# A decode step with adaLN: the closing rows in two column groups, with two plain stores

## The chip, the cores and the metric

The kernel runs on one core of a Trainium2 chip. The metric is device time of one execution in microseconds (us), taken over several executions of each kernel; lower is better. A profiled execution of each kernel gives a trace. The span of a profile (84 us here) is shorter than the device time (85.7 us) by what lies before the first and after the last instruction.

## The reference

One token for each of four sequences goes through an attention block with a key and value cache and through a feed-forward block, both with an adaptive layer norm:

```python
mod = (silu(c) @ w_mod).reshape(4, 6, 1, 512)              # sa, ca, ga, sb, cb, gb
h = layernorm(x) * (1 + ca) + sa
x = x + ga * attention(h, k_cache, v_cache, wq, wo)        # 32 heads, window of 1024 keys
h = layernorm(x) * (1 + cb) + sb
x = x + gb * (relu(h @ w1) @ w2)                           # w1: 512 x 1792, w2: 1792 x 512
```

The output is 4 x 512 in bf16, 4 KB. The inputs that have to be read are 32 MB.

## The kernel before

The change concerns the last line of the reference. The sum over 1792 is cut in 14 blocks of 128 (block m, `w2_sb[:, m, :]`), and w2 arrives in five loads, of 4, 4, 3, 2 and 1 blocks. The activation of a block, `uT32[:, m, :]`, is a 128 x 32 weight tile with the four sequences in columns 0, 8, 16 and 24 and zeros between. Each block takes four matmuls, one in each group of 32 columns of the array; group g makes output columns 128 g to 128 g + 127 and leaves them on partitions 32 g to 32 g + 31.

```python
CG = 32; NH = 4; DH2 = 128; BS = 8
W2_CHUNKS = [(0, 4), (4, 4), (8, 3), (11, 2), (13, 1)]
...
def ffn2(m0, m1):
    for m in range(m0, m1):
        for nh in range(NH):
            nc.tensor.matmul(out=z_ps[nh * CG:(nh + 1) * CG, :], lhsT=uT32[:, m, :],
                             rhs=w2_sb[:, m, nh * DH2:(nh + 1) * DH2],
                             start=(m == 0), stop=(m == FT - 1), tile_position=(0, nh * CG))
...
nc.vector.tensor_tensor(out=zg[:], in0=z_ps[:], in1=gb2[:], op=ALU.mult)
nc.vector.tensor_tensor(out=res[:], in0=zg[:], in1=x12_ps[:], op=ALU.add)
nc.scalar.dma_start(out=out.rearrange("b o (g n) -> (o g) b n", g=NH), in_=res[::BS, :])
```

So the 16 rows to be stored lie on every eighth partition, and their places in the output need two dimensions, [4 groups, 4 sequences], beside the 256 bytes of a row.

## Time and profile before

| | before |
|---|---|
| device time, median of the first 3 runs | 85.74 us (85.63 to 85.79) |
| span of the profile | 84.19 us |
| last landing of w2 | 80.62 us |
| last matmul ends | 80.96 us |
| store issued, landed | 81.66 us, 83.36 us |

The first two rows are the whole; the other three are single records of the trace and cut the piece that the change can touch. The page's clock row belongs to it, since the last matmuls run at the throttled clock (each digit is a fortieth of the span, in tenths of full speed):

```profile
PEclk9999999999996555599999999559755555555555
```

And these are the w2 matmuls of the kernel before in order of time (start, duration, engine, line, what, count, idle time before and what ended it):

```profile
78.25 1.10 PE L472 MATMUL z_ps<-w,uT 128*32 128x128 bf16 x32 [0.21 <-DVE uT L467]
...
79.66 0.51 PE L472 MATMUL z_ps<-w,uT 128*32 128x128 bf16 x12 [0.31 <-DMA w<-in_B_w_dram]
...
80.33 0.64 PE L472 MATMUL z_ps<-w,uT 128*32 128x128 bf16 x12 [0.15 <-DMA w<-in_B_w_dram]
```

The reader is to see the gaps: the tensor engine is through with what has landed and waits for the next load of w2 (0.31 us, then 0.15 us).

### The profile page before, as it was taken

The numbers are of one execution on the slowest core, as the hardware profiler recorded it, in microseconds if no ns is written. First come the engines' busy times: TensorE is split into PE (matmuls) and PEld (weight loads), VectorE is DVE, ScalarE is ACT, GpSimd is POOL, SyncE is SP. The second block draws the span as 40 slices with busy tenths as digits, with TensorE's granted clock in tenths as the row PEclk, the third lists the DMA queues.
The fourth block names the chain that finished last, engine by engine and source line by source line (L and its number), as shares of the span: only waits on it lengthen the run. The fifth ranks groups of instructions, "written<-read, shape, count | busy, mean of one in ns | idle before, by whom it ended". The sixth has DMA issues, their size and how long they took to land.

```text
span 84.2 us, 2368 instructions
## 1 busy us (share of the span) xinstructions
PE 56.2 (67%) x1064; PEld 47.2 (56%) x1064; DVE 25.7 (31%) x73; ACT 23.6 (28%) x37; POOL 5.2 (6%) x20
## 2 busy tenths in 40 slices
PE   0001006999972889999999941999727579598730
PEld 0000006996772883997777801999727239588610
DVE  0104000348133100164665476950001320251320
ACT  2301001664302000487788718640100010001000
POOL 6980000000000000000000000000000000000000
PEclk9999999999996555599999999559755555555555
DMA  2799999999989999999999999999999999999500
GB/s 31 301 457 455 386 432 471 459 483 420 389 370 405 424 424 424 401 428 424 409 420 420 420 420 416 416 424 428 409 416 424 416 415 432 418 387 399 186 1 2
DMA packets 4221, 32.14 MB, mean 382 GB/s; under 512 B 492, under 2 KB 628, under 8 KB 1268
## 3 DMA queue, kind: packets, MB, share of 16 engines
q1 hardware_dynamic: 4176, 31.98, 91.7%
q8 instruction: 8, 0.13, 0.6%
q10 hardware_dynamic: 36, 0.01, 0.1%
q14 instruction: 1, 0.01, 0.0%
HBM read 31.99 MB, written 0.00 MB: 380 GB/s over the span
## 4 chain that ended last, share of the span: by engine, by line
DMA 93%; SPq 2%; PE 1%; DVE 1%; issue 0%
DMA v<-in_A_v_cache_dram 33%; DMA wo_sb<-in_A_wo_dram 24%; DMA w<-in_B_w_dram 19%; DMA k<-in_A_k_cache_dram 16%; PE z_ps L472 1%; SPq L81 1%; SPq L91 0%; SPq L90 0%; DVE zg L482 0%; DVE res L484 0%
## 5 line engine op out<-in xcount | busy, mean ns | idle before, releaser
L204 PE MATMUL ktp<-ident_k,k 128*128 128x128 bf16 x256 | 19.1, 247 | 6.5 <-DMA k<-in_A_k_cache_dram 6.5
L204 PEld LDWEIGHTS <-k 128*128 128x128 bf16 x256 | 18.1, 113 | 9.1 <-DMA k<-in_A_k_cache_dram 6.6
L209 ACT COPY kT<-ktp 128x1024 bf16<-128x1024 bf16 x16 | 15.6, 1015 | 19.0 <-PE ktp L204 18.0
L207 DVE COPY kT<-ktp 128x1024 bf16<-128x1024 bf16 x16 | 11.1, 692 | 18.0 <-PE ktp L204 17.7
L342 PE MATMUL oT_ps<-pT,v 128*128 128x16 bf16 x256 | 7.1, 172 | 2.0 <-issue 2.0
L342 PEld LDWEIGHTS <-v 128*128 128x128 bf16 x256 | 7.0, 100 | 2.1 <-issue 2.0
L216 PE MATMUL sc_ps<-kT,qpad 128*32 128x512 bf16 x64 | 5.6, 445 | 0.4 <-DVE qpad L308 0.4
L359 PE MATMUL pT_ps<-ident_bf,p_rep 128*128 128x128 bf16 x32 | 3.2, 282 | 2.9 <-DVE p_rep L353 2.9
L179 PE MATMUL tp<-ident_bf,cx_sb 8*128 8x8 bf16 x4 | 0.3, 169 | 6.6 <-DMA cx_sb<-in_A_x_dram 6.6
L359 PEld LDWEIGHTS <-p_rep 128*128 128x128 bf16 x32 | 2.8, 131 | 3.4 <-DVE p_rep L353 3.4
L304 PE MATMUL qT_ps<-hT,wq_sb 128*128 128x4 bf16 x128 | 3.5, 166 | 1.4 <-DVE ab L297 1.4
L304 PEld LDWEIGHTS <-wq_sb 128*128 128x128 bf16 x128 | 3.5, 104 | 1.5 <-issue 1.5
L179 PEld LDWEIGHTS <-cx_sb 8*128 8x128 bf16 x4 | 0.2, 112 | 6.6 <-issue 6.6
L411 ACT COPY y<-y_ps 128x256 f32<-128x256 f32 x1 | 0.4, 372 | 9.3 <-DVE y L410 9.3
L353 DVE TENSOR_TENSOR p_rep<-e_sb,mi 128x512 int32<-128x512 int32 x4 | 2.5, 687 | 0.7 <-ACT e_sb L348 0.7
L472 PE MATMUL z_ps<-w,uT 128*32 128x128 bf16 x56 | 2.2, 303 | 0.7 <-DMA w<-in_B_w_dram 0.5
L384 DVE TENSOR_TENSOR oT_sb<-oT_ps,rb 128x128 bf16<-128x128 f32 x1 | 0.3, 291 | 7.8 <-PE oT_ps L342 7.8
L418 PEld LDWEIGHTS <-wo_sb 128*128 128x128 bf16 x64 | 2.5, 120 | 0.4 <-DMA wo_sb<-in_A_wo_dram 0.4
L418 PE MATMUL y_ps<-o,wo_sb 128*128 128x4 bf16 x64 | 2.4, 173 | 0.3 <-DMA wo_sb<-in_A_wo_dram 0.3
L414 PEld LDWEIGHTS y_ps<-sel_b,y 128*128 128x128 f32 x8 | 1.8, 327 | 1.4 <-DVE y L410 1.4
L406 PE MATMUL y_ps<-wo_sb,o 128*32 128x512 bf16 x16 | 1.9, 628 | 0.9 <-DVE o L397 0.9
L216 PEld LDWEIGHTS <-qpad 128*32 128x32 bf16 x64 | 1.3, 103 | 2.2 <-DVE qpad L308 0.7
(107 smaller groups left out, 51.9 us busy)
## 6 DMA issues: line engine op xcount, KB each, us to landing
k<-in_A_k_cache_dram SPq DMA_DIRECT2D x8, 1024.0 KB, 28.1
v<-in_A_v_cache_dram SPq DMA_DIRECT2D x8, 1024.0 KB, 20.1
wq_sb<-in_A_wq_dram SPq DMA_DIRECT2D x1, 4096.0 KB, 22.5
wo_sb<-in_A_wo_dram SPq DMA_DIRECT2D x4, 1024.0 KB, 20.4
wmod_sb<-in_w_mod_dram SPq DMA_DIRECT2D x1, 2304.0 KB, 9.7
w<-in_B_w_dram SPq DMA_DIRECT2D x1, 1792.0 KB, 21.9
w<-in_B_w_dram SPq DMA_DIRECT2D x2, 512.0 KB, 19.5
wmod_sb<-in_w_mod_dram SPq DMA_DIRECT2D x1, 768.0 KB, 4.6
```

The lines of the kernel that those rows point to most:

```text
L204: nc.tensor.transpose(out=tp[:, ii, :], in_=k_tiles[gi][:, iq * IQ + ii, :], identity=ident_k)
L207: nc.vector.tensor_copy(out=dst, in_=tp[:])
L209: nc.scalar.copy(out=dst, in_=tp[:])
L216: nc.tensor.matmul(out=sc_ps[hw * CG:(hw + 1) * CG, half * HALF:(half + 1) * HALF], lhsT=qpad[:, b, par, hw, :], rhs=kT[:, half * (NI // 2 ...
L304: nc.tensor.matmul(out=qT_v[:, hq, :], lhsT=wq_sb[:, t, hq * Dh:(hq + 1) * Dh], rhs=hT[:, t, :], start=(t == 0 and hq == 0), stop=(t == DT ...
L342: nc.tensor.matmul(out=oT_ps[:, hw, par].rearrange("p b r -> p (b r)"), lhsT=v_tiles[h][:, i, :], rhs=pT[:, i, c0:c0 + B * rep], start=(fi ...
L353: nc.vector.tensor_tensor(out=p_w[:, ws, :], in0=e_w[:, ws].unsqueeze(2).to_broadcast([P, WQ // 2, B]), in1=mi4[:].unsqueeze(1).to_broadca ...
L359: nc.tensor.transpose(out=tp[:, ii, :], in_=p_rep[:, i // 2, :, i % 2], identity=ident_bf[:])
L406: nc.tensor.matmul(out=y4_ps[q0:q0 + CG, :], lhsT=o4[:, l, g % 2, g // 2, :], rhs=wo_sb[:, g, l, :], start=(g == 0 and l < 4), stop=(g == ...
L414: nc.tensor.matmul(out=y_ps[:, t, :], lhsT=y4[:, t, :], rhs=sel_b[:], start=(t == 0), stop=False)
L418: nc.tensor.matmul(out=y_ps[:, m, :], lhsT=wo_sb[:, g, l, m::DT], rhs=o4[:, l, g % 2, g // 2, 0:B], start=False, stop=(g == NP - 1 and l = ...
L472: nc.tensor.matmul(out=z_ps[nh * CG:(nh + 1) * CG, :], lhsT=uT32[:, m, :], rhs=w2_sb[:, m, nh * DH2:(nh + 1) * DH2], start=(m == 0), stop= ...
```

## The change

The intent is a cheaper store. If a group's 32 columns hold the four sequences at columns 0, 2, 4, 6 once and at 1, 3, 5, 7 once (the same tile, read from one column earlier: windows x = 0 and 1), the group can make two output quarters on interleaved, adjacent partitions. Two groups then suffice, the result lies on partitions 0 to 7 and 32 to 39, and two stores with plain patterns, one on SP's queue and one on ACT's, take it out. To make up for the two idle groups, blocks 0 to 3 of w2 go to the upper two groups, beside blocks 4 to 7 in the lower ones, and their part is copied, scaled and added to the residual ahead of time (zc). The core of the diff; the same windows are used for gb and x12 earlier, which is cut here:

```diff
-    siluT32 = const.tile([P, DT, CG], bf16, name="siluT32")
+    siluT32 = const.tile([P, DT, CP], bf16, name="siluT32")       # CP = CG + 2; uT32 and xs2 likewise
+    def rows(tile3, j, x):
+        return tile3[:, j, NX - x:NX - x + CG]                    # NX = 2
+    def closing(parts):
+        for x in range(NX):
+            for (ps, q, j, src, rhs, start, stop, cols) in parts:
+                for g in range(2):
+                    q0 = (q + g) * CG
+                    nc.tensor.matmul(out=ps[q0:q0 + CG, cols], lhsT=rows(src, j, x), rhs=rhs(2 * x + g),
+                                     start=start and x == 0, stop=stop and x == NX - 1, tile_position=(0, q0))
 ... (cut)
-    for (m0, e) in W2_CHUNKS:
-        ffn2(m0, m0 + e)
+    for m in range(ZA):                                           # ZA = 4
+        closing([zpart(m), zpart(ZA + m)])                        # upper groups beside lower groups
+    zc = work.tile([2 * CG, DH2], f32, name="zc")
+    nc.scalar.copy(out=zc[:], in_=za_ps[2 * CG:P, :])
+    nc.vector.tensor_tensor(out=zc[:], in0=zc[:], in1=gb2[:], op=ALU.mult)
+    nc.vector.tensor_tensor(out=zc[:], in0=zc[:], in1=x12_ps[:], op=ALU.add)
+    for m in range(2 * ZA, FT):
+        closing([zpart(m)])
 ... (cut)
-    nc.vector.tensor_tensor(out=res[:], in0=zg[:], in1=x12_ps[:], op=ALU.add)
-    nc.scalar.dma_start(out=out.rearrange("b o (g n) -> (o g) b n", g=NH), in_=res[::BS, :])
+    nc.vector.tensor_tensor(out=res[:], in0=zg[:], in1=zc[:], op=ALU.add)
+    out_v = out.rearrange("b o (x g n) -> (b o x) g n", x=NX, g=2)
+    nc.sync.dma_start(out=out_v[:, 0, :], in_=res[0:NX * B, :])
+    nc.scalar.dma_start(out=out_v[:, 1, :], in_=res[CG:CG + NX * B, :])
```

## The prediction

> **What bounds the kernel now.** I read the page's engine shares first, then its slices, then the chain that ended last in order of time, and last the trace of the final four microseconds. No engine is full, so the bound is not a compute engine:
>
> ```profile
> PE 56.2 (67%) x1064; PEld 47.2 (56%) x1064; DVE 25.7 (31%) x73; ACT 23.6 (28%) x37; POOL 5.2 (6%) x20
> ...
> DMA  2799999999989999999999999999999999999500
> ...
> HBM read 31.99 MB, written 0.00 MB: 380 GB/s over the span
> ```
>
> The DMA row stands at 9 from the third slice to the thirty-seventh: the kernel streams 32 MB of caches and weights, and everything else lies beside that stream. The chain says the same and shows what lies outside:
>
> ```profile
> 64.37 15.92 DMA w<-in_B_w_dram
> 80.28 0.04 issue
> 80.33 0.66 PE z_ps L472 x11
> 80.99 0.02 issue
> 81.01 0.30 DVE zg L482
> 81.31 0.02 issue
> 81.34 0.29 DVE res L484
> ```
>
> Up to 80.28 us the chain is DMA alone. So a change of this kernel that reads the same bytes can pay only in the piece from the last landings of w2 to the end at 84.2 us, about 4 us of 84. The reader is to see that line 472's matmuls, two vector instructions and the store follow each other there, nothing beside them. The store and the wait for it take most of it:
>
> ```profile
> 81.66 0.60 ACTq L485 DMA_DIRECT2D out_dram<-res  x1
> ```
>
> ```profile
> SPq L511 <- DMA out_dram<-res: 1.6, 1, 1.6
> ```
>
> The second line is from the waits of the DMA queue's engine: it waits 1.6 us for the store, up to 83.37; the remaining 0.8 us, to 84.19, is the closing hand-shake of the engines, which the change doesn't touch. From single records: the last five loads of w land at 77.39, 78.69, 79.62, 80.28 and 80.62 (issue time plus time to landing: the last is 66.85 plus the 13.8 of the page's DMA part). The matmuls wait for the last one, start at 80.66 and end at 80.96; zg runs 81.01 to 81.30, res 81.34 to 81.62; the store is issued from 81.66 to 82.26, its first packet starts at 82.91, its last at 83.02, and it has landed at 83.36.
>
> **What the Trainium skill says.** (1) "TensorE: Matmul & The Clock Gate", "Wait — 56ns, not 53.3ns?": at the throttled clock matmuls follow each other every N / 1.2 GHz, 106.7 ns for 128 columns. The trace agrees: in this stretch the granted clock is 0.50, and in the run of line 472 from 78.25 rounds of four matmuls (one in each column group) start 105 to 107 ns apart. (2) Same page, "Part 3: Packing small matmuls", "The mechanism": matmuls at different tile positions run beside each other, about 4 ns apart. The trace agrees: the four of a round start within 3 to 16 ns. So a column group takes one matmul in 107 ns, and with two groups in use the array has half the throughput of four. (3) "VectorE: DVE Perf Modes", section on the TRN2 errata: an fp32 tensor-tensor instruction takes (N+151)/0.96 ns, and that does not depend on how many partitions it covers. At N = 128 this is 291 ns; zg took 292 and res 287. (4) "DMA: Bandwidth & Descriptors", "Why a DMA increments its semaphore by 16 and not by 1": the number of DMA engines is the largest common divisor, up to 16, of the two patterns' slowest dimensions. The store's [4,4] destination makes it 4, and its 16 packets of 256 bytes indeed come four to an engine; five semaphore events (one for the unused twelve, four landings) agree. An [8] by 256 byte store should use 8 engines with one packet each.
>
> **The change, part by part.** In the front part little is at stake. The widened zero tiles and the small copy ident_m cost 0.2 us of DVE and some ns of POOL, both idle there until 6.6 us. Gb's 16 matmuls in two groups cost PE at most some 0.3 us in the early stage, and x12 keeps its 16 matmuls; the loads are issued 14 to 28 us before they land, so such a shift leaves the stream as it is. After x12, PE waits for w1 anyway (landed 76.12, first u matmul 76.17; x12 ended at 75.74), a slack of 0.4 us. These parts: 0.
>
> W2's first 32 matmuls (blocks 0 to 3 beside 4 to 7) use all four groups again, so the pace is the same; but the first pair needs the second chunk, landed 78.69, where before it was needed only half-way. Eight rounds by 107 ns from 78.73 end their starts at 79.59, just ahead of the third chunk (79.62, start 79.66): 0, with no slack left. The ACT copy of za_ps (gb's like copy took 251 ns) and two vector instructions (about 290 each) begin near 79.9 and are over by 80.8, ahead of zg: 0.
>
> From block 8 on only two groups work, and here the change loses. Blocks 8 to 10 are 12 matmuls = 6 rounds by 107 ns: 79.66 to 80.30, about when the fourth chunk lets PE go on (80.33). Blocks 11 and 12 are 4 rounds, not 2; from the spacing of the trace (the second round of a burst follows after about 65 ns, the later ones after 107) the next round could start at about 80.71, after the last landing and its 80.66. The last block takes 2 rounds and not 1: 80.71 + 0.107 + 0.31 (one matmul's record) = 81.13, against 80.96. **PE on the path: +0.17 us.**
>
> The final vector pair is unchanged in length: same 128 columns, half the partitions, zc from SBUF in place of x12_ps; the trace's 128x16 instructions take 174 ns from either memory. So 0, and res ends near 81.79.
>
> The stores: the old one is issued on ACT in 602 ns with the pattern [4,4]. SP's issues show what a second dimension costs: loads of k and v, pattern [1,128], take 535 ns, wo and w, pattern [128,1], take 328. ACT's second load at the start, [4,1], took 265. I take 328 on SP and 265 to 400 on ACT, side by side: −0.27 us. Then the packets: four to an engine from 82.91 to 83.02 become one to an engine and queue, −0.06 us (estimate from 18 ns a packet and 11 to 15 ns spacing). One more semaphore to await at the end: +0.03. **Stores on the path: −0.30 us.** Sum: 0.17 − 0.30 = −0.13 us, span 84.06, time 85.74 − 0.13 = **85.6 us**.
>
> **The rivals.** (a) The issue does not get cheaper. For it: ACT's very first issue, also two-dimensional, took 568 ns, and at that moment SP was issuing too; if it was the simultaneous issue or the long pause of the queue that made it slow, the ACT store will take 0.57 again. Against: SP's issue at that same moment took 374, little over its 328. Then only −0.03 and −0.06 + 0.03 remain, and with PE's +0.17 the time is 85.8 to 85.9. (b) PE's loss is larger: weights of both windows go to the same two groups, and if a weight load can't hide behind a matmul of its own group, a round takes more than 107 ns. The trace speaks against it (four groups each took a new weight load in every 107 ns round), but with the 12 + 8 + 4 matmuls of the last six blocks each 10 ns costs 0.12 us: 86.0. (c) PE's loss is hidden. If the last landing comes later than 80.71 in a typical run, the queue of earlier blocks is empty by then and only one extra round (0.107) is left: 85.5. (d) The landing of a 4 KB store is dominated by its receipt, 0.35 us after the last packet and 0.65 between issue and first packet, so the finer split gains nothing beyond the issue: 85.7. A gain in the stream is no rival: same bytes, same order of loads.
>
> **Range and chances.** The pieces run from −0.40 (stores all gained, PE half hidden) to +0.25 (issue not cheaper and PE's loss full). Runs of the kernel before spread by 0.16 us, another chip may shift all by a tenth or two. I take 85.2 to 86.0. Two per cent is 1.7 us, nearly half of the whole closing piece that the change can touch; no chain of these pieces comes near. Within 2%: 0.97; faster 0.02; slower 0.01.
>
> **What would show it.** Right: the last landing within 0.1 us of 80.6; line 194's last z_ps matmul ending 0.45 to 0.55 us after that landing (0.34 before); the records of the last six blocks in rounds of two, 107 ns apart; zg and res still about 290 ns; two store issues starting within 50 ns of each other, both under 0.4 us; one data packet to an engine and queue; end of span 0.82 us after the later landing. Wrong: an issue near 0.57 or 0.6 us on ACT (rival a); rounds of more than 115 ns (b); last z_ps matmul starting 43 ns after the landing (c); zc's sum ending after the last matmul, which would put ACT and DVE on the path; a wait of the u matmuls for x12 in place of w1.

## The result, and the profile after

The changed kernel takes 85.81 us (median of 6 runs, 85.68 to 85.95), the kernel before 85.73 us in the same rounds (6 runs, 85.61 to 85.98). Ratios here are the mean time of one kernel's fast runs over that of the other's of the same rounds, so not quite the ratio of the medians; this one is 1.0007, with a 95% interval of 0.9989 to 1.0025: the same.

The chain of the changed kernel in order of time, its last pieces:

```profile
79.44 1.48 PE z_ps L194 x26
80.95 0.29 DVE zg L504
81.27 0.28 DVE res L506
```

Where the chain of the kernel before came from DMA to a burst of 11 matmuls of 0.66 us, it now ends in 1.48 us of matmuls whose records leave no gap: the tensor engine has become the last link in this stage. A matmul's record lasts 0.31 us, so records overlap and hide short waits. By the starts of the single records the engine still waited for the fourth load, which landed at 80.045 and was used from 80.086; the six rounds from there to the end wait for nothing. (Further up this chain goes through PE from 13 to 39 us, where the other went through DMA. That is a matter of which of two waits ended last; the DMA row of the page is full there in both kernels, and w2's last landing is at 80.36 us, no later than before.) The timeline of the same piece:

```profile
79.22 1.68 PE L194 MATMUL z_ps<-w,uT 128*32 128x128 bf16 x26
...
79.49 0.26 ACT L497 COPY zc<-za_ps 64x128 f32<-64x128 f32 x1 [3.57 <-PE za_ps L194]
79.78 0.28 DVE L498 TENSOR_TENSOR zc<-zc,gb 64x128 f32<-64x128 f32 x1 [1.31 <-ACT zc L497]
80.10 0.28 DVE L499 TENSOR_TENSOR zc<-zc,x_ps 64x128 f32<-64x128 f32 x1
80.95 0.28 DVE L504 TENSOR_TENSOR zg<-z_ps,gb 64x128 f32<-64x128 f32 x1 [0.57 <-PE z_ps L194]
81.27 0.28 DVE L506 TENSOR_TENSOR res<-zg,zc 64x128 bf16<-64x128 f32 x1
81.58 0.37 SPq L508 DMA_DIRECT2D out_dram<-res  x1
81.58 0.30 ACTq L509 DMA_DIRECT2D out_dram<-res  x1
```

To see: zc is ready at 80.38, well ahead of zg at 80.95, where VectorE waits for the tensor engine; the two issues start together and take 0.37 and 0.30 us in place of 0.60. So the store side is cheaper, as intended. The total did not move because two things took it back. I cut the piece after the last landing of w2 in five parts, from single records of the traces:

| us | last landing of w2 to last matmul's end | to the first store's issue | to the last store's landing | to SP's first closing drain | to the end | sum |
|---|---|---|---|---|---|---|
| before | 0.342 | 0.693 | 1.699 | 0.083 | 0.751 | 3.568 |
| changed | 0.544 | 0.666 | 1.397 | 0.248 | 0.750 | 3.605 |
| difference | +0.202 | −0.027 | −0.302 | +0.165 | −0.001 | +0.037 |

The third column is what the change is for. The first is the price at the tensor engine. The fourth was not foreseen at this size: after its store has landed, SP works through a fixed sequence of waits for all semaphores of the kernel, mostly two to an instruction. In the kernel before the store's semaphore is in the last of these; the changed kernel has one DMA more, which moves SP's store to the third, so that three further waits, about 0.06 us each, run after the landing: the wait for SP's store ends at 82.995 us, three more start at 83.031, 83.093 and 83.152, and the drain at 83.220 (single records of the trace, which no view prints).

The last landing itself moves from run to run (80.10 to 80.62 us over the profiles, with no relation to the kernel that I can see), and so the times scatter by some 0.3 us. The five parts are steadier: the kernels that share a part agree in it within 0.03 us, but for D where the stores' semaphores are the last two (waits_last). I use the parts for the mechanism and the ratios for the whole.

### The profile page after: what moved, and what is told of

It is laid out like the page before. It is cut to its first block, busy times and chain, and to the rows that moved or that the text cites. A ratio compares the mean times of both kernels' runs of the same rounds, so it can differ in the third digit from the quotient of the medians.

```text
span 84.0 us, 2373 instructions
## 1 busy us (share of the span) xinstructions
PE 55.5 (66%) x1064; PEld 46.5 (55%) x1064; DVE 26.5 (32%) x76; ACT 23.8 (28%) x38; POOL 5.3 (6%) x20
## 4 chain that ended last, share of the span: by engine, by line
DMA 60%; PE 30%; DVE 3%; issue 1%; SPq 1%; ACT 1%; DVEq 0%
DMA v<-in_A_v_cache_dram 24%; DMA w<-in_B_w_dram 23%; DMA k<-in_A_k_cache_dram 14%; PE ktp L225 14%; PE qT_ps L322 4%; PE sc_ps L237 3%; PE z_ps L194 3%; PE mT L273 2%; PE mT L275 1%; PE m_ps L259 1%; PE m_ps L262 1%; PE st_ps_var L289 1%; PE gb_ps L194 1%; SPq L93 0%; SPq L92 0%
## 5 line engine op out<-in xcount | busy, mean ns | idle before, releaser
L225 PE MATMUL ktp<-ident_k,k 128*128 128x128 bf16 x256 | 17.8, 237 | 7.5 <-DMA k<-in_A_k_cache_dram 7.5
L225 PEld LDWEIGHTS <-k 128*128 128x128 bf16 x256 | 16.8, 108 | 10.1 <-DMA k<-in_A_k_cache_dram 7.5
L194 PEld LDWEIGHTS <-uT 128*32 128x32 bf16 x56 | 2.2, 136 | 0.8 <-DMA w<-in_B_w_dram 0.4
```

Source lines behind the costliest of these rows:

```text
L194: nc.tensor.matmul(out=ps[q0:q0 + CG, cols], lhsT=rows(src, j, x), rhs=rhs(2 * x + g), start=start and x == 0, stop=stop and x == NX - 1, ...
L225: nc.tensor.transpose(out=tp[:, ii, :], in_=k_tiles[gi][:, iq * IQ + ii, :], identity=ident_k)
```

## The experiments

Twelve runs followed the first result; waits_again is the kernel of waits_last once more. This is the same cut for each, one profiled execution each; the texts below refer to its columns as A to E. The diffs are shortened in places, and say so:

| us | A: landing to matmul's end | B: to store's issue | C: to store's landing | D: to SP's drain | E: to the end | sum | ratio to before (95%) |
|---|---|---|---|---|---|---|---|
| before | 0.342 | 0.693 | 1.699 | 0.083 | 0.751 | 3.568 | 1 |
| changed | 0.544 | 0.666 | 1.397 | 0.248 | 0.750 | 3.605 | 1.0007 (0.9989 to 1.0025) |
| late4 | 0.339 | 0.657 | 1.387 | 0.247 | 0.745 | 3.375 | 0.9962 (0.9940 to 0.9984) |
| lower_only | 0.815 | 0.665 | 1.391 | 0.247 | 0.745 | 3.863 | 1.0045 (1.0019 to 1.0071) |
| waits_last | 0.548 | 0.667 | 1.380 | 0.143 | 0.745 | 3.483 | 0.9973 (0.9954 to 0.9993) |
| before_2x3d | 0.342 | 0.688 | 1.920 | 0.247 | 0.751 | 3.948 | 1.0043 (1.0017 to 1.0069) |
| one_store | 0.540 | 0.665 | 1.187 | 0.084 | 0.745 | 3.221 | 0.9960 (0.9936 to 0.9985) |
| both_act | 0.543 | 0.668 | 1.534 | 0.248 | 0.744 | 3.737 | 1.0034 (1.0002 to 1.0067) |
| before_joined | 0.338 | 0.691 | 1.725 | 0.143 | 0.745 | 3.642 | 1.0010 (0.9987 to 1.0034) |
| chunks_last | 0.853 | 0.664 | 1.384 | 0.084 | 0.751 | 3.736 | 1.0006 (0.9984 to 1.0028) |
| chunks_fine | 0.838 | 0.673 | 1.391 | 0.084 | 0.750 | 3.736 | 1.0005 (0.9988 to 1.0023) |
| waits_again | 0.555 | 0.665 | 1.384 | 0.084 | 0.745 | 3.433 | 0.9975 (0.9958 to 0.9992) |
| before_4x2d | 0.338 | 0.689 | 2.773 | 0.395 | 0.750 | 4.945 | 1.0155 (1.0137 to 1.0173) |
| pattern_split | 0.550 | 0.668 | 2.064 | 0.248 | 0.750 | 4.280 | none: one run, 86.71 us, state unknown |

### late4: four column groups to the end (wrong)

```diff
     for m in range(2 * ZA, FT):
-        closing([zpart(m)])
+        for x in range(NX):
+            for g in range(2):
+                j = 2 * x + g; q0 = j * CG        # window 1 goes to the upper groups of zb_ps, never read
+                nc.tensor.matmul(out=(zb_ps if x else z_ps)[q0:q0 + CG, :], lhsT=rows(uT32, m, x), ...)   # (cut)
```

> The changed kernel, but from block 8 on the second window's matmuls go to the two upper column groups of a tile that nobody reads: four groups stay in use to the end. The result is wrong on purpose; the stores, the vector work and the closing waits are those of the changed kernel. Theory (the two-group matmuls lose, the stores win back as much): from the last landing of w2 to the end of the last matmul 0.34 us as in the kernel before, in place of 0.54; the piece from last landing to the end of the span 3.40 us in place of 3.60; time about 0.2 us under the changed kernel, near 85.6. Rival (the matmuls' pace is not what lengthened this piece, but later weight loads or the start of the last block): it stays above 0.45 us and the time stays at 85.8.

The last z_ps matmuls of this kernel, and the vector instruction that follows them:

```profile
80.02 0.29 PE L506 MATMUL z_ps<-w,uT 128*32 128x128 bf16 x2 [0.17 <-DMA w<-in_B_w_dram]
...
80.31 0.29 PE L506 MATMUL z_ps<-w,uT 128*32 128x128 bf16 x2
...
80.64 0.28 DVE L510 TENSOR_TENSOR zg<-z_ps,gb 64x128 f32<-64x128 f32 x1 [0.35 <-PE zb_ps L506]
```

The engine waits for the fourth load again (0.17 us), and the last load, landed at 80.267, is used from 80.31 on. A is 0.339 us, the kernel before's 0.342; the sum falls by 0.230 to 3.375, and the time to 85.41 us, lower than the 85.6 expected. The number of matmuls and weight loads is that of the changed kernel, only the groups differ. So the 0.2 us is the pace of two groups, and the rest of the change, taken alone, gains.

### lower_only: without the early upper groups

```diff
-        upper = m < ZA
+        upper = False        # (cut: the tile za_ps goes, start and stop are m == 0 and m == FT - 1)
-    for m in range(ZA):
-        closing([zpart(m), zpart(ZA + m)])
-    ... zc ...
-    for m in range(2 * ZA, FT):
+    for m in range(FT):
         closing([zpart(m)])
-    nc.vector.tensor_tensor(out=res[:], in0=zg[:], in1=zc[:], op=ALU.add)
+    nc.vector.tensor_tensor(out=res[:], in0=zg[:], in1=x12_ps[:], op=ALU.add)
```

> The changed kernel without its early upper groups: all 14 blocks of w2 in the two lower groups, no za_ps, zc and copy, the sum with x12 from PSUM as before. Theory (a group takes one matmul in 107 ns): the 56 matmuls are 28 rounds from about 78.0, 3.0 us, so the last one starts near 80.95 and ends near 81.25, 0.3 to 0.35 us later than in the changed kernel after the same landings; time about 86.1. Rival (PE catches up, since it waits for w2 anyway): the last matmul ends as in the changed kernel, time 85.8.

The timeline of this kernel, its w2 matmuls:

```profile
78.05 3.17 PE L194 MATMUL z_ps<-w,uT 128*32 128x128 bf16 x56 [0.16 <-DVE uT L484]
```

All 56 matmuls in one run, with no wait for w2 in between: 28 rounds by 107 ns are 3.0 us, plus the drain of the last. A grows by 0.271 us against the changed kernel and the time to 86.19 us. This is what the second half of the change, blocks 0 to 3 in two more groups, is worth: it keeps the engine from falling further behind.

### waits_last: the stores' semaphores at the end of the closing waits

```diff
-    for g in range(NP):
-        nc.sync.dma_start(out=wo_dst[:, g, :], in_=wo_src[:, g, :])
+    for (g0, g1) in [(0, 2), (2, 3), (3, 4)]:
+        nc.sync.dma_start(out=wo_dst[:, g0:g1, :], in_=wo_src[:, g0:g1, :])
```

One DMA fewer in the program shifts the eight semaphores, which are dealt out in turn, by one, so that the two stores get the last two. (The order of the two store lines does not decide this: ACT's store has the eighth semaphore and SP's the first in the changed kernel, where SP's line comes first, and in before_2x3d, where ACT's does.)

> The changed kernel with the first two loads of wo joined into one, so that the two stores' semaphores are the last two in the sequence of closing waits (before the join SP's store is awaited third, with three more waits after it). Theory (these waits are done one after the other, some 0.06 us each, after the later landing): from the later landing to the first closing drain of SP 0.08 us in place of 0.25; the end of the span 0.16 us sooner after the last landing of w2 (3.44 in place of 3.60 us); time about 85.65. Rival (the time after the landing is of the two-queue store itself): 0.25 us again, time 85.8. The joined load itself should move nothing, as wo's first half has long landed when it is needed.

D falls from 0.248 to 0.143 us; it isn't 0.083, because in this run ACT's store landed after SP's and its semaphore is the last but one. The time is 85.54 us, ratio 0.9973: shorter than both kernels. The sum explains 0.12 us of it against the changed kernel and 0.09 us against the kernel before.

### before_2x3d: the old layout with the store cut in two

```diff
-    nc.scalar.dma_start(out=out.rearrange("b o (g n) -> (o g) b n", g=NH), in_=res[::BS, :])
+    out_g = out.rearrange("b o (g n) -> (o g) b n", g=NH)
+    nc.scalar.dma_start(out=out_g[2:4], in_=res[2 * CG:4 * CG:BS, :])
+    nc.sync.dma_start(out=out_g[0:2], in_=res[0:2 * CG:BS, :])
```

> The kernel before with its one store cut in two halves of two column groups each, pattern [2,4] by 256 bytes, one on ACT and one on SP. Theory (an issue costs more because the pattern has a further dimension): each issue takes 0.5 to 0.6 us, as loads with a further dimension did on SP (0.535), and nothing is won in issuing; with two packets to an engine and two more closing waits after SP's landing the time is 85.75 to 85.9. Rival (an issue costs by the number of its pieces, 16 in the old store, 8 in the new ones): issues of 0.35 to 0.4 us, and the time is 85.6, without any loss on the tensor engine.

The issues of this kernel in its timeline:

```profile
81.24 0.67 SPq L487 DMA_DIRECT2D out_dram<-res  x1
81.25 0.60 ACTq L486 DMA_DIRECT2D out_dram<-res  x1
```

Half as many pieces to an issue, and each issue as dear as the whole old one: the number of pieces is not what costs. With the later landing and the further waits the kernel is slower than before (86.09 us). Two queues alone buy nothing; the pattern does.

### one_store: half of the output (wrong)

```diff
-    nc.scalar.dma_start(out=out_v[:, 1, :], in_=res[CG:CG + NX * B, :])
```

> The changed kernel with the first of its two stores alone, on SP; half of the output is never written, so the result is wrong on purpose. In the traces so far, of two stores issued together the one whose packets start first lands 1.19 to 1.21 us after the issue and the other 1.38 to 1.40, whichever queue it is on. Theory (the second store of the shared engines is held up by the first): the single store lands 1.20 us after its issue; with its semaphore the last of the closing waits (0.08 us) the piece from the last landing of w2 to the end is 0.54 + 0.67 + 1.20 + 0.08 + 0.75 = 3.24 us in place of 3.60. Rival (SP's queue or its 0.36 us issue lands later by itself): 1.39 us, and 3.44 us in all.

```profile
81.77 0.36 SPq L508 DMA_DIRECT2D out_dram<-res  x1
```

The issue takes as long as beside a second one (0.35 to 0.37 us). A store alone lands 1.187 us after its issue starts. Of two issued together one lands after 1.19 to 1.21 us and the other after 1.38 to 1.40, on whichever queue it is: SP's in the changed kernel, ACT's in waits_last. So the second store costs 0.2 us in C by being there, and nearly all of it lies behind the last packet: from there to the landing the store alone takes 0.330 us, the first of two (ACT's in the changed kernel) 0.332 and the later one 0.503. The landing events show that each uses eight DMA engines (one event for the unused eight at once, then eight landings), and the packets of the second start only 0.03 us after those of the first. The Trainium skill, "DMA: Bandwidth & Descriptors", "Queues, rings and completion order", says that the write which counts up the semaphore lands only after every earlier write of that DMA engine, across its queues. The measured 0.2 us agrees with it if both stores sit on the same engines; no run here shows by itself which engines they use.

### both_act: both stores on one queue

```diff
-    nc.sync.dma_start(out=out_v[:, 0, :], in_=res[0:NX * B, :])
+    nc.scalar.dma_start(out=out_v[:, 0, :], in_=res[0:NX * B, :])
```

> The changed kernel with both stores issued on ACT, one after the other. Theory (issues on one queue follow each other, so that the second queue is what lets the second store in at the same time): the second issue starts 0.34 us after the first and its landing comes about 1.5 us after the first issue (0.34 + 1.20), in place of 1.40; its semaphore is awaited third, as in the changed kernel; time about 0.12 us over the changed kernel, 85.9. Rival (the landing of the second store is bound by the shared engines in any case, 0.19 after the first): 1.40 again and 85.8.

```profile
81.31 0.29 ACTq L508 DMA_DIRECT2D out_dram<-res  x1
81.64 0.31 ACTq L509 DMA_DIRECT2D out_dram<-res  x1
```

C is 1.534 us: 0.334 to the second issue and 1.200 from there. Set apart by a third of a microsecond the second store is not held up by the first; it only starts late. The four runs read 85.76, 85.86, 86.35 and 86.38 us, a wider scatter than elsewhere, and the ratio (1.0034) is uncertain to the same degree; the sum says 0.13 us over the changed kernel.

### before_joined: the joined load alone

The edit is that of waits_last, on the kernel before.

> The kernel before with the first two loads of wo joined, and nothing else: the control for the run with the waits at the end, which was 0.29 us faster than the changed kernel while the piece after the last landing was only 0.12 us shorter. The store's semaphore becomes the last but one of the closing waits. Theory 1 (the joined load leaves the stream alone, the rest was the stream's scatter): the piece after the last landing is 3.57 + 0.06 = 3.63 us and the time 85.75 to 85.85. Theory 2 (the joined load also makes the stream end sooner by 0.15 us): time about 85.65.

85.84 us against 85.79, ratio 1.0010, sum 3.642: the joined load does not make the stream end sooner, and the one further closing wait shows as 0.060 us in D. Theory 1 holds.

### chunks_last: other loads of w2

```diff
-    W2_CHUNKS = [(0, 4), (4, 4), (8, 3), (11, 2), (13, 1)]
+    W2_CHUNKS = [(0, 4), (4, 4), (8, 4), (12, 1), (13, 1)]          # on waits_last
```

> The run with the waits at the end, and w2 loaded in chunks of 4, 4, 4, 1 and 1 blocks in place of 4, 4, 3, 2 and 1, so that only two rounds of matmuls, not four, stand between the last landing but one and the last. Theory (of the 0.20 us that the tensor engine lost, some 0.06 to 0.09 is the queue of blocks 11 and 12, the rest the one extra round of the last block): from the last landing to the last matmul's end 0.45 us in place of 0.55, the piece to the end of the span 3.39 in place of 3.48; [...]time 85.45 to 85.5. Rival (the pace of the last block itself is the whole loss): 0.55 again, time 85.55.

A miss: A is not 0.45 but 0.853 us. The timeline tells why:

```profile
79.56 1.46 PE L194 MATMUL z_ps<-w,uT 128*32 128x128 bf16 x24 [0.20 <-DMA w<-in_B_w_dram]
```

Blocks 8 to 11 land together, at 79.51, where in waits_last blocks 8 to 10 landed at 79.14. From there the last six blocks, 12 rounds by 107 ns, run without a gap, so the end is set by when the first of them could start. I had looked at the last two loads alone; a queue that begins earlier is as bad.

### chunks_fine: finer loads at the end, one coarse one ahead

```diff
-    W2_CHUNKS = [(0, 4), (4, 4), (8, 3), (11, 2), (13, 1)]
+    W2_CHUNKS = [(0, 8), (8, 2), (10, 2), (12, 1), (13, 1)]         # on waits_last
```

> The run with the waits at the end, with w2 in chunks of 8, 2, 2, 1 and 1 blocks. The coarser chunks of the run before this one made the tensor engine start blocks 8 to 11 late (landing 79.51) and be behind for all that followed. Theory (what counts is that the engine, at 0.21 us a block in two groups against 0.32 us a block of the stream, has no block waiting when the last one lands): with landings 1.28, 0.64, 0.32 and 0 us before the last, blocks 8 and 9 are done long before 10 and 11 land, those end 0.16 us after block 12 has landed, and the engine has caught up when the last lands; from there to the last matmul's end 0.45 us in place of 0.55, the piece to the end 3.38 to 3.44; time 85.4 to 85.5. Rival (another cost of small chunks, in the stream, eats it): 85.55 or more at the same piece.

A miss again, A 0.838 us, with another cause. Blocks 8 and 9 had landed at 79.01, in good time, but the w2 matmuls began only at 78.84 us and never stopped. The stage before them, the w1 matmuls, was slower. Its weight loads (shortest, median and longest in ns), first in the changed kernel:

```profile
L479 PEld LDWEIGHTS <-w x56: 103/117/132, 75.9 to 77.6; 128*128 128x128 bf16 x56
```

and in chunks_fine:

```profile
L479 PEld LDWEIGHTS <-w x56: 104/170/175, 75.9 to 78.5; 128*128 128x128 bf16 x56
```

The kernel reads w1's columns with a step equal to the size of the w2 chunk, so that the rows of a chunk come out in one piece. A step of 8 elements (16 bytes) makes a weight load take 171 ns in place of 118 at a step of 4 (8 bytes) and 104 at steps of 1 to 3, and 32 of these loads lie ahead of the w2 matmuls. The Trainium skill, "SBUF — State Buffer", "Door 1: The DMA port swizzle", states that the memory has lines of 16 bytes and that full bandwidth needs at least two accesses to a line. The jump from 118 to 171 ns, where a step of 16 bytes leaves one access to a line, agrees with that; the 118 ns at two accesses to a line, over the 104, do not quite. The same passage gives 8 bf16 elements as how far one can stride for free, which the 171 ns at a step of 8 contradict. That the lines are the cause is not shown. So the size of the queue's share in A stays untested by a kernel of its own; the records of the changed kernel put it at 0.06 us (see the tensor engine's step in the account below).

### waits_again: the shortest kernel once more

> The run with the waits at the end again, the same kernel: whether its lead over both kernels holds on another chip and beside the finer chunks. By its piece of 3.48 us, against 3.57 of the kernel before and 3.60 of the changed one, it should lead the kernel before by 0.1 us and no more; it led by 0.27. Expected 85.6 to 85.7 with the kernel before at 85.75, ratio 0.998 to 0.999.

85.53 us against 85.78, ratio 0.9975 (0.9958 to 0.9992), on another chip than the first time. D is 0.084 us here, SP's store having landed last. The lead is confirmed, at 0.25%; by the sums it should be 0.1 to 0.16% (0.09 and 0.135 us of 85.75), which lies within the interval. Whether the rest is anything but scatter stays open: in all four runs that have the joined load on the changed kernel the ratio says 0.08 to 0.15 us less than the sum, but in late4, without that load, it says 0.13 less too, and in before_joined, with it, nothing of the kind.

### before_4x2d: the plain pattern without the two-group layout

```diff
-    nc.scalar.dma_start(out=out.rearrange("b o (g n) -> (o g) b n", g=NH), in_=res[::BS, :])
+    for g in range(NH):
+        (nc.scalar if g % 2 == 0 else nc.sync).dma_start(
+            out=out[:, 0, g * DH2:(g + 1) * DH2], in_=res[g * CG:(g + 1) * CG:BS, :])
```

> The kernel before with four stores of one column group each, pattern [4] by 256 bytes, two on ACT and two on SP: the cheap pattern without the two-group layout. Theory (issues of one queue follow each other, each about 0.3 to 0.37 us): the last landing is 1.6 to 1.8 us after the first issue, about where the single [4,4] store lands (1.70), and two to three more closing waits follow; piece 3.65 to 3.8, time 85.8 to 86.0. Rival (small stores overlap better than that): 1.5 us or less, and the two-group layout was not needed.

Far slower than expected, 87.11 us. The issues:

```profile
81.44 1.49 SPq L486 DMA_DIRECT2D out_dram<-res  x2
81.44 1.34 ACTq L486 DMA_DIRECT2D out_dram<-res  x2
```

That is 0.60 to 0.75 us for each of four issues (single records), although each has two dimensions only, four rows of 256 bytes. The reading of the prediction, that the further dimension makes an issue dear, can't be the whole: these stores read every eighth partition, and that may be enough by itself. The next run takes the two apart.

### pattern_split: which part of the pattern costs (wrong on purpose, one look)

```diff
-    nc.sync.dma_start(out=out_v[:, 0, :], in_=res[0:NX * B, :])
-    nc.scalar.dma_start(out=out_v[:, 1, :], in_=res[CG:CG + NX * B, :])
+    out_x = out.rearrange("b o (x g n) -> g x (b o) n", x=NX, g=2)
+    nc.sync.dma_start(out=out_x[0], in_=res[0:NX * B, :])           # adjacent partitions, [2,4] in the output
+    nc.scalar.dma_start(out=out_v[:, 1, :], in_=res[::8, :])        # every eighth partition, [8] in the output
```

> The changed kernel with its two stores told apart, wrong on purpose. SP's store reads the same eight adjacent partitions but writes its rows in an order that needs a further dimension in the output, [2,4] by 256 bytes; ACT's store keeps its two-dimensional output [8] and reads every eighth partition of 64. Measured so far on SP and ACT: 0.35 to 0.37 and 0.29 to 0.30 us with adjacent partitions and two dimensions; 0.67 and 0.60 to 0.62 with every eighth partition and three dimensions; but also 0.69 to 0.75 and 0.60 to 0.70 with every eighth partition and two dimensions. Theory of the prediction (the further dimension costs): SP 0.55 to 0.67, ACT 0.30. Theory 2 (the step between partitions costs): SP 0.36, ACT 0.60 or more. Both may hold, then both are near 0.6.

```profile
81.77 0.77 SPq L509 DMA_DIRECT2D out_dram<-res  x1
81.77 0.67 ACTq L510 DMA_DIRECT2D out_dram<-res  x1
```

Both are dear. A further dimension with adjacent partitions takes 0.77 us on SP, a step between partitions with two dimensions 0.67 us on ACT. The issue of a store was cheap (0.29 to 0.37 us) only where neither was there. One doubt remains: the two ran at the same time, so that the one could have slowed the other. For the step, before_4x2d shows it in all four issues without any further dimension. For the dimension the loads say two things: those of k and v on SP (0.535 against 0.328 us), which ran alone, point the same way, but the joined load of wo in waits_last, with a further dimension of 2, took only 0.388. So a further dimension made this store dear; that it always costs as much is not so.

What comes next goes with the pattern too. From the end of an issue on a free queue to its first packet it is 0.42 to 0.50 us for the plain stores, but 0.65 on ACT and 0.86 to 0.89 on SP for every store with a step or a further dimension (before, before_joined, before_2x3d, before_4x2d, pattern_split). With that, C is 2.064 us here against 1.397, and the single run took 86.71 us against 85.85 (one run each, states unknown).

## Why the prediction was right or wrong

The range (85.2 to 86.0) held 85.81, and "the same" was right. The point, 85.6, was 0.2 us low: a gain of 0.13 us was summed up, and there is none. By its own steps:

- **Only the piece after the last landings counts.** Right. Gb's matmuls in two groups spread over 1.03 us in place of 0.81, and nothing later moved for it; the u matmuls still waited for w1 (0.71 us), not for x12.
- **Blocks 0 to 7: no loss, no slack.** Right. The first pair waited for the second load (0.23 us), and the third load's blocks began at 79.42, just after it landed at 79.38.
- **zc off the path.** Right: ready 0.57 us before zg.
- **PE +0.17 us.** Right in mechanism, measured +0.202; late4 shows that it is the groups, and the engine was 0.06 us behind at the last landing (its block began at 80.465, the landing was at 80.365 and the usual start 0.043 later), about as worked out (0.05). Rivals (b) and (c) fall: rounds were 107 ns apart, and the loss wasn't hidden.
- **Vector pair: 0.** Measured −0.027 us for B, with 284 and 282 ns in place of 292 and 287 for half the partitions.
- **Stores −0.30 us.** The sum of this step failed, and the term that failed is "One more semaphore to await at the end: +0.03": it was +0.165 us. With it fell the reading that the last 0.8 us are a hand-shake "which the change doesn't touch", and the sign that the span ends 0.82 us after the later landing (it was 1.00). I counted one further wait; what matters is how many waits stand behind the one for the later landing, three of 0.06 us. waits_last and before_joined show it directly. The rest of the step, −0.33 us from issue to landing, measured −0.302, but by other terms than I gave: the issue −0.235 (0.602 to 0.367; rival (a) falls), the time between the end of the issue and the first packet −0.20 (0.647 on ACT to 0.445 on SP), which I had taken as fixed and which goes with the pattern (pattern_split), the packets −0.03, and the landing after the last packet +0.17, which one_store puts down to the second store. So rival (d), which takes both of these times as given, falls too. Two errors cancelled, and that −0.33 is so near to −0.302 is luck.
- **The cause of the cheap issue** was half right: the further dimension costs, but so does the step between partitions, which the prediction did not name. It also passed over the load of wq, pattern [128,1] like wo, whose issue took 672 ns.
- **Slips in the working.** The ends of the pieces, −0.40 and +0.25, don't come out of the terms (−0.30 + 0.09 = −0.21 and 0.17 − 0.06 = +0.11); 86.0 in rival (b) would take some 33 ns more a round, not 10; and the four matmuls of a round start within 30 ns, not 16, from 78.79 on. The last landing, 80.365, was not within 0.1 us of 80.6. None of this changes the result.

With the term at its measured size the sum is 0.202 − 0.027 − 0.302 + 0.165 = +0.04 us, with which the ratio of 1.0007 (0.06 us of 85.75) agrees; its interval, some 0.15 us to either side, is too wide to prove the sum, and the predicted −0.13 us lies just outside it. What the stores and the vector pair gain, 0.33 us, is taken back by the tensor engine (0.20), which pays for the layout that makes the store cheap, and by a sequence of waits after the landing (0.165).

## What to carry to other kernels

Where a stream of loads bounds a kernel, cut the piece after its last landing into landing, last matmul, store issue, store landing and closing waits: parts of 0.1 us are plain there while the whole scatters by 0.3 us. A small last store was cheapest here with adjacent partitions and a two-dimensional pattern, and the end came soonest with the semaphore of the last landing last in the closing waits; neither costs anything where the layout allows it. A layout that uses half of the column groups was paid for with the engine's pace in the blocks that land last, so weigh it against the store there, and move the earlier blocks to the idle groups as this change does.

## What the Trainium skill lacked or had wrong

- "DMA: Bandwidth & Descriptors" does not give the issue time by pattern: 0.29 to 0.37 us for eight adjacent partitions in two dimensions, 0.60 to 0.75 with every eighth partition, 0.77 with adjacent partitions and a further dimension in the output. Nor the time from there to the first packet: 0.42 to 0.50 us for the first kind, 0.65 to 0.89 for the others.
- The same page does not give the cost of a second small store issued at the same time: 1.19 us from issue to landing alone, 1.38 to 1.40 for the later of two.
- No page has the closing sequence: waits for the semaphores one after the other, 0.06 us each, in a fixed order, so that a store's place in it moves the end by up to 0.165 us here; then 0.75 us to the end of the span.
- "TensorE: Matmul & The Clock Gate" gives a weight load's time by its columns alone; it was 104, 118 and 171 ns for 128 columns at steps of up to 3, of 4 and of 8 bf16 elements. The lines of 16 bytes on "SBUF — State Buffer" fit the largest of these, but that page gives 8 bf16 elements as how far one can stride for free, and the 171 ns at a step of 8 are not.
- Where the pages were used for the prediction (107 ns a round at the throttled clock, about 290 ns for the vector instructions) the runs agreed (rounds of 106 to 107 ns; 278 to 292 ns).
